# Block 0 of a fused sparse-attention and feed-forward kernel: a written list of steps in place of due times, and local outputs joined by row

## The chip, the core and the metric

The kernel runs on one core of a Trainium2 chip, in one launch. The metric is the device time of that launch in microseconds, as the median of several runs. Lower is better. The engines are PE (matrix products, transposes), DVE and ACT (elementwise work, copies out of PSUM, exponentials), POOL (masks at the start) and SP, whose queue issues nearly all transfers. Each engine works through its own list of instructions in order and waits where an operand isn't ready.

## The reference

Attention over 8 batches, 8 heads, 576 positions and 64 dimensions, with a local mask in half the heads and a strided one in the other half; the heads are joined to rows of 512 and go through a feed-forward layer with a SiLU gate.

```python
rel = pos[:, None] - pos[None, :]
mask_local = (rel >= 0) & (rel < 32)
mask_strided = (rel >= 0) & (pos[None, :] % 32 == pos[:, None] % 32)
masks = np.stack([mask_local if h < H // 2 else mask_strided for h in range(H)], axis=0)
scores = np.where(masks, q @ k.T / 8, -1e9)
attn = softmax(scores)                  # along the keys
x = (attn @ v).transpose(0, 2, 1, 3).reshape(4608, 512)
h = x @ w_in                            # 512 x 2048
g = h * (1.0 / (1.0 + np.exp(-h)))
return g @ w_out                        # 2048 x 512
```

All of it is float32.

## The kernel before

**Blocks and chunks.** The 4608 rows of x go in 9 blocks of 512 columns (x is held transposed: 128 partitions are two heads of 64). For each block the hidden layer goes in 16 chunks of 128. A chunk is 12 products into one PSUM bank (`hidden`, four column pieces of x times three pairings) and 12 into the four output banks (`output`). Three pairings, since each float32 operand is split into a rounded high half and the rest (`w` high and low, `xhi` and `xlo`, `ghi` and `glo`), and high times high, high times low and low times high are added up. A chunk's hidden bank goes through a tanh on ACT and a gate on DVE, and then through its own split.

**Attention groups.** Each batch is cut into six groups: three local ones (12 tiles of 32 queries against 64 keys, two heads) and three strided ones (8, 8 and 6 tiles). Group numbers run on: 0 to 5 make the x of batch 0, 6 to 11 that of batch 1, and so on. A group's steps are: load k and q (`k`), scores on PE (`S`), masked peak on DVE (`M`), exponentials with row sums on ACT (`E`), row sums inverted on DVE (`R`), scaling on DVE (`N`), transposes on PE (`T`), a copy out of PSUM (`P`), load v (`v`), values on PE (`O`), a copy into x (`B`). In the trace, exponentials are L425, peaks L416, scaling L437, transposes L443, values L472, scores L398.

**Block 0 is special.** While the first block of the feed-forward layer runs, the kernel must also load all weights and split them (32 pieces of 256 or 512 KB: `p` load, `a` two roundings on ACT, `j` join on DVE, `b` high half by DVE or ACT, `d` low half on DVE), make the x of batch 0 and batch 1 and score groups 12 and 13. Chunk fc of block 0 has steps `h` and `i` (the two halves of `hidden`), `t` (tanh), `g` (gate), `w` and `l` (high and low half of the gated value), `o` (`output`). `H` and `L` split x into `xhi` and `xlo`: H00 to H03 for block 0, H10 to H13 for block 1. All these steps are put into lists for the engines by a planner that runs when the program is built, not on the chip.

**The planner.** Each step has a cost per engine that may do it, a due time, steps that it comes after, and rings of buffers that it takes. `Steps.arrange` repeats: take the steps that could start, keep those that start within 0.05 of the earliest, and choose the one with the least due time; the engine is the one on which the step would end first. Where PE would stand idle, `keep_warm` adds transposes of the identity (L664) whose results nobody reads. Due times are formulas, such as

```python
outs = [attention_steps(c, (5 + 2.4 * c, 9 + 2.4 * c, 11 + 2.4 * c, 13 + 2.4 * c))
        for c in range(NG)]
begin, pace = 24.0, 6.4
```

**Blocks 1 to 8** are written as a plain loop over chunks: `hidden`, `silu`, the `output` of the chunk before, and at three chunks of a block `products`, which computes the values of two groups and the scores of the two groups behind them. There the transposes are done by DVE in blocks (`turn_by_blocks`, L462), not by PE. For block 1 the three chunks are 2, 6 and 11, for the later ones 1, 6 and 11; groups 12 and 13 are normalised and turned in chunks 0 and 1 of block 1 (`following`). `store` scales the four output tiles of a block by 0.5 and writes them out.

## Time and profile before

| | |
|---|---|
| time, median of 3 runs | 888.8 us (888.44 to 888.88) |
| the profiled execution | 889.7 us, its span 887.6 us |
| PE busy | 876.9 us (99%) |
| DVE busy | 509.1 us (57%) |
| ACT busy | 314.2 us (35%) |
| HBM read, written | 54.00 MB, 9.44 MB |
| first product of h0 (PE, L554) | starts at 29.50 us |
| first products of block 1 (PE, L554) | start at 135.77 us in the chain |

The profile is one execution. Its span is 2.1 us shorter than the time of that execution, which holds the launch's beginning and end too. PE's busy time counts overlapping products, so 99% does not mean that every product runs at its best. An engine's idle time is named with what ended it, and only idle time on the way to the last instruction makes the kernel longer.

### The profile page before, as it was taken

The numbers are of one execution on the slowest core, as the hardware profiler recorded it, in microseconds if no ns is written. First come the engines' busy times: TensorE is split into PE (matmuls) and PEld (weight loads), VectorE is DVE, ScalarE is ACT, GpSimd is POOL, SyncE is SP. The second block draws the span as 40 slices with busy tenths as digits, with TensorE's granted clock in tenths as the row PEclk, the third lists the DMA queues.
The fourth block names the chain that finished last, engine by engine and source line by source line (L and its number), as shares of the span: only waits on it lengthen the run. The fifth ranks groups of instructions, "written<-read, shape, count | busy, mean of one in ns | idle before, by whom it ended". The sixth has DMA issues, their size and how long they took to land.

```text
span 887.6 us, 18081 instructions
## 1 busy us (share of the span) xinstructions
PE 876.9 (99%) x7283; PEld 722.0 (81%) x7283; DVE 509.1 (57%) x1602; ACT 314.2 (35%) x1059; POOL 5.8 (1%) x28
## 2 busy tenths in 40 slices
PE   8999999999999999999999999999999999999998
PEld 7777788888888887888888888888788888888886
DVE  5999757666476566458556656655654433343333
ACT  6989643333333333314413432333331221121111
POOL 2000000000000000000000000000000000000000
PEclk9999999999999999999999999999999999999999
DMA  8886513122122202202301221221200010001001
GB/s 267 280 272 222 164 45 111 58 71 76 49 68 71 75 36 81 71 1 75 116 7 64 76 70 46 71 75 48 68 29 1 1 48 1 0 1 48 1 0 48
DMA packets 37043, 64.60 MB, mean 73 GB/s; under 512 B 2912, under 2 KB 23776, under 8 KB 36960
## 3 DMA queue, kind: packets, MB, share of 16 engines
q1 hardware_dynamic: 36000, 62.60, 21.6%
q8 instruction: 57, 0.93, 0.4%
q10 hardware_dynamic: 960, 0.85, 0.3%
q14 instruction: 26, 0.21, 0.1%
HBM read 54.00 MB, written 9.44 MB: 71 GB/s over the span
## 4 chain that ended last, share of the span: by engine, by line
PE 90%; DVE 5%; DMA 3%; ACT 1%; issue 0%; SPq 0%; ACTq 0%; DVEq 0%
PE po L600 42%; PE ps L554 41%; PE ps L398 3%; PE ps L487 3%; DMA stage<-w_in 2%; DMA stage<-w_out 1%; DVE stage L293 1%; DVE w L337 1%; PE ps L472 1%; PE po L472 1%; DVE w L333 0%; PE ps L664 0%; DVE glo L580 0%; DMA k<-kqt 0%; DVE th L568 0%
## 5 line engine op out<-in xcount | busy, mean ns | idle before, releaser
L554 PE MATMUL ps<-xhi,w 128*128 128x512 f32 x1152 | 378.1, 391 | 0.1
L568 DVE SCALAR_TENSOR_TENSOR th<-th,ps 128x512 f32<-128x512 f32 (+1 forms) x147 | 99.3, 676 | 272.7 <-ACT th L564 272.6
L554 PEld LDWEIGHTS ps<-xhi,w 128*128 128x128 f32 x1152 | 216.3, 188 | 45.6 <-DVE w L337 0.4
L564 ACT ACTIVATE th<-ps 128x512 f32<-128x512 f32 (+1 forms) x147 | 86.5, 588 | 455.1 <-PE ps L554 448.8
L554 PE MATMUL ps<-xlo,w 128*128 128x512 f32 x576 | 224.2, 389 | 0.0
L600 PE MATMUL po<-w,ghi 128*128 128x512 f32 x504 | 157.1, 393 | 0.4 <-DVE ghi L576 0.4
L554 PEld LDWEIGHTS ps<-xlo,w 128*128 128x128 f32 x576 | 108.1, 188 | 22.0
L600 PEld LDWEIGHTS po<-w,ghi 128*128 128x128 f32 x504 | 93.5, 188 | 20.4 <-ACT stage L287 0.8
L425 ACT ACTIVATE sm<-sm,sums 128x64 f32<-128x64 f32 x320 | 106.4, 338 | 3.1 <-DVE sums L416 3.1
L580 DVE TENSOR_TENSOR glo<-th,ghi 128x512 fp32r<-128x512 f32 (+1 forms) x147 | 100.0, 681 | 11.8
L600 PE MATMUL po<-w,glo 128*128 128x512 f32 x252 | 98.5, 391 | 1.6 <-DVE sums L416 0.9
L600 PE MATMUL po<-stage,ghi 128*128 128x512 f32 x288 | 88.7, 389 | 0.0
L600 PE MATMUL po<-v,ghi 128*128 128x512 f32 x216 | 67.3, 393 | 0.1
L576 DVE CAST ghi<-th 128x512 fp32r<-128x512 f32 (+1 forms) x140 | 59.0, 422 | 11.8
L600 PEld LDWEIGHTS po<-stage,ghi 128*128 128x128 f32 x288 | 54.1, 188 | 11.2
L425 ACT ACTIVATION_READ_ACCUMULATOR sm<-sm,sums 128x1 f32 x320 | 61.4, 192 | 0.0
L462 DVE STREAM_TRANSPOSE pt<-sm 32x192 f32<-32x192 f32 (+1 forms) x144 | 56.4, 392 | 2.6
L600 PEld LDWEIGHTS po<-w,glo 128*128 128x128 f32 x252 | 47.3, 188 | 12.9 <-DVE glo L580 1.7
L600 PE MATMUL po<-stage,glo 128*128 128x512 f32 x144 | 56.0, 389 | 0.0
L600 PEld LDWEIGHTS po<-v,ghi 128*128 128x128 f32 x216 | 40.1, 188 | 8.8 <-issue 0.3
L600 PE MATMUL po<-k,ghi 128*128 128x512 f32 x144 | 44.4, 390 | 0.0
L600 PE MATMUL po<-v,glo 128*128 128x512 f32 x108 | 42.2, 391 | 0.2 <-DVE glo L580 0.2
(72 smaller groups left out, 664.6 us busy)
## 6 DMA issues: line engine op xcount, KB each, us to landing
out<-stage SPq DMA_DIRECT2D x36, 256.0 KB, 2.0
v<-vt SPq DMA_DIRECT2D x21, 384.0 KB, 5.4
k<-kqt SPq DMA_DIRECT2D x14, 512.0 KB, 4.8
stage<-w_out SPq DMA_DIRECT2D x14, 512.0 KB, 4.2
stage<-w_in SPq DMA_DIRECT2D x12, 512.0 KB, 4.5
k<-kqt SPq DMA_DIRECT2D x14, 416.0 KB, 4.0
v<-vt SPq DMA_DIRECT2D x14, 256.0 KB, 5.0
k<-kqt SPq DMA_DIRECT2D x7, 448.0 KB, 3.9
```

The source lines that it names most:

```text
L293: nc.vector.scalar_tensor_tensor(out=upper, in0=upper, scalar=3, in1=lower, op0=ALU.logical_shift_left, op1=ALU.bitwise_or,)
L398: nc.tensor.matmul(self.pss[h][rows, c * KW : (c + 1) * KW], kbd[at, 1, g.q0[t] : g.q0[t] + g.rows], kbd[at, 0, g.k0[t] : g.k0[t] + KW], s ...
L425: nc.scalar.activation(out=self.s_sb[:, c, h], in_=self.s_sb[:, c, h], func=AF.Exp, bias=self.peaks[:, c, h : h + 1], scale=-1.0, accum_ou ...
L462: nc.vector.transpose(out=pt[to, r % 2], in_=src[rows, 1 - r % 2])
L472: nc.tensor.matmul(self.pso[h * D : (h + 1) * D, t * size : (t + 1) * size], vbd[at, t], moved, start=True, stop=True,)
L487: nc.tensor.matmul(self.pso[p][h * D : (h + 1) * D, i * size : (i + 1) * size], vbd[at, 2 * i + h], moved, start=True, stop=True,)
L554: nc.tensor.matmul(ph, weight(0, wi, fc)[:, cc * P : (cc + 1) * P], x[xi][cc], start=(cc, n) == (0, 0), stop=(cc, n) == (NP - 1, 2),)
L564: nc.scalar.activation(out=th[:, cols], in_=ph[:, cols], func=AF.Tanh, scale=0.5)
L568: nc.vector.scalar_tensor_tensor(out=th[:, cols], in0=th[:, cols], scalar=1.0, in1=ph[:, cols], op0=ALU.add, op1=ALU.mult,)
L576: copy[engine](out=g[0][:, cols], in_=th[:, cols])
L580: nc.vector.tensor_sub(out=g[1][:, cols], in0=th[:, cols], in1=g[0][:, cols].bitcast(F32))
L600: nc.tensor.matmul(po[tt], g[gi][:, cols], weight(1, wi, fc), start=fc == 0 and n == 0, stop=fc == NFC - 1 and n == 2,)
```

## The change

**A written list.** A string `PLAN` names the 439 steps of block 0 in an order, some with an engine behind a dot (`P0.D` is DVE, `P4.A` is ACT). A new method `follow` makes each step's place in the list its due time and takes away the other engines. `arrange` then runs as before; on each engine the steps come out in the list's order. The planner's costs for PE's fillers rise (0.27 to 0.34 up to time 12 rather than 9), so that fewer are put in: 29 transposes instead of 75.

**Local outputs by row.** In batches 0 and 1 the exponentials of local groups are no longer scaled (`N` goes for them). The values step puts queries on PSUM partitions, with one bank for each head, stationary 32 columns of `pt` and moving 64 columns of `vbd`. A new step `Q` (`share`) multiplies the two banks by the inverted sums on DVE into an SBUF tile `xq`; `X` (`back`) turns it on PE with three transposes; `B` copies it into x.

**Smaller edits.** Groups 12 and 13 are normalised and turned in the list (`V12`, `V13`), and the first `products` of block 1 comes at chunk 1. The second half of `v0` is issued by SP, not ACT. In the last block's `store`, even tiles are scaled whole by DVE and odd ones whole by ACT, where before each was cut in two halves. The dependences of `h`, `i`, `o`, `H` and of lent buffers are written out more fully, since due times no longer imply them.

```diff
+PLAN = """
+k0 k1 k2 S0 M0 k4 S1 E0 M1 v0 S2 M2 k3 E1 T0 S4 P0.D R0 v1 M4 E2 O0 T1 Q0 k5 P1.D X0 R1 S3 E4
...
+H12.A j31 H13.D b31.A L12 L13 d31 i15 o14 t15 g15 w15.D l15
+"""
...
-COLD, WARM = 0.27, 0.14
-WARM_FROM, WARM_UNTIL = 9.0, 60.0
+COLD, WARM = 0.34, 0.14
+WARM_FROM, WARM_UNTIL = 12.0, 60.0
...
+    def follow(self, plan):
+        for i, word in enumerate(plan.split()):
+            name, _, engine = word.partition(".")
+            step = self[name]
+            step.due = i
+            step.costs = {e: c for e, c in step.costs.items() if e.startswith(engine)}
...
         def values(self):
             g, pt, vbd = self.g, self.pt, self.vbd
-            self.pso, size = self.bank("pso"), STRIDE if g.local else SEQ
+            if g.local:
+                self.pso = [self.bank("pso") for _ in range(2)]
+            else:
+                self.pso = self.bank("pso")
             for t, c, rows in self.tiles:
                 r = rows.start // STRIDE
                 for h in range(2):
                     at = slice(h * KW, (h + 1) * KW)
-                    moved = pt[at, c, r] if g.local else pt[at, c, r : r + 2, :HALF]
-                    nc.tensor.matmul(
-                        self.pso[h * D : (h + 1) * D, t * size : (t + 1) * size],
-                        vbd[at, t], moved, start=True, stop=True,
-                    )
+                    if g.local:
+                        nc.tensor.matmul(
+                            self.pso[h][rows, c * D : (c + 1) * D],
+                            pt[at, c, r], vbd[at, t], start=True, stop=True,
+                        )
+                    else:
+                        nc.tensor.matmul(
+                            self.pso[h * D : (h + 1) * D, t * SEQ : (t + 1) * SEQ], vbd[at, t],
+                            pt[at, c, r : r + 2, :HALF], start=True, stop=True,
+                        )
...
+        def share(self):
+            g = self.g
+            self.xq = att.tile([P, 3 * P], F32, name="xq", bufs=1)
+            o_sb = self.xq.rearrange("p (c h d) -> p c h d", h=2, d=D)[:, : g.n]
+            for h, o_ps in enumerate(self.halves(self.pso)):
+                inv = self.rsum[:, :, h].unsqueeze(2).broadcast_to([P, g.n, D])
+                nc.vector.tensor_mul(o_sb[:, :, h], o_ps, inv)
+        def back(self):
+            self.psx = self.bank("psp")
+            for c in range(self.g.n):
+                at = slice(c * P, (c + 1) * P)
+                nc.tensor.transpose(self.psx[:, at], self.xq[:, at], ident)
...
-            half = DM if k < NBLK - 1 else DM // 2
-            nc.scalar.mul(out=osb[:, :half], in_=po[tt][:, :half], mul=0.5)
-            if half < DM:
-                nc.vector.tensor_scalar_mul(osb[:, half:], po[tt][:, half:], 0.5)
+            if k == NBLK - 1 and tt % 2 == 0:
+                nc.vector.tensor_scalar_mul(osb, po[tt], 0.5)
+            else:
+                nc.scalar.mul(out=osb, in_=po[tt], mul=0.5)
...
-        soft = add(f"N{c}", {"DVE": 0.08 + 0.13 * n}, t1 - 1, [r], a.scale)
+        soft = e
+        if not local or a.b >= EARLY:
+            soft = add(f"N{c}", {"DVE": 0.08 + 0.13 * n}, t1 - 1, [r], a.scale)
         if last == "S":
+            t = add(f"V{c}", {"DVE": 0.85 + 0.45 * n}, t1, [soft], a.turn_by_blocks, takes=["pt"])
...
         if local:
-            d = add(f"B{c}", {"ACT": 0.38, "DVE": 0.47}, t2 + 1, [o],
-                    lambda: a.done(d.engine), gives=[o])
+            q = add(f"Q{c}", {"DVE": 0.53}, t2 + 0.5, [o, r], a.share, takes=["xq"], gives=[o])
+            x = add(f"X{c}", {"PE": 0.1 + 0.12 * n}, t3 + 0.01, [q], a.back, takes=[mid])
+            d = add(f"B{c}", {"ACT": 0.38, "DVE": 0.47}, t3 + 1, [x], lambda: a.done(d.engine),
+                    gives=[x])
...
+    steps.follow(PLAN)
     for step in steps.arrange():
         step.act()
...
-        plan[(b - 1) * NFC + (1 if b > 2 else 2, 6, 11)[at // 2]] = c
+        plan[(b - 1) * NFC + (1, 6, 11)[at // 2]] = c
...
-    for i in range(2):
-        group = groups[2 * NG + i]
-        following[NFC + i] += [lambda g=group: normalize(g), group.turn_by_blocks]
```

In the rows that follow, `sm` holds a group's exponentials, `po` and `ps` are PSUM banks, `pt` turned exponentials, `xb` x, `stage` a weight piece; `x18` at the end counts equal rows. ACT at the start of the program, before (L425 exponential, L525 and L447 copies of local outputs and of turned exponentials, L542 a half of x, L519 a strided output, L282 the first rounding of weights):

```order
L425 ACTIVATE sm,sums<-sm,sums 128x64 x18
L525 COPY xb<-po 128x384
L447 COPY pt<-po 128x384
L425 ACTIVATE sm,sums<-sm,sums 128x64 x8
L525 COPY xb<-po 128x384
L542 CAST xhi<-xb 128x512
L425 ACTIVATE sm,sums<-sm,sums 128x64 x14
L519 COPY xb<-po 128x24x18
L282 ACTIVATE stage_468<-stage_468 128x512
```

and with the change (L453 exponential, L475, L579 and L563 the copies, L312 and L317 the roundings):

```order
L453 ACTIVATE sm,sums<-sm,sums 128x64 x40
L475 COPY pt<-po 128x512
L312 ACTIVATE stage_456<-stage_456 128x512
L317 ACTIVATE stage_456<-stage_456 128x512
L579 COPY xb<-po 128x3x4x32
L563 COPY xb<-po 128x8x18
L563 COPY xb<-po 128x15x18
L475 COPY pt<-po 128x384
L312 ACTIVATE stage_537<-stage_537 128x512
```

The 40 exponentials of the first six groups stood in three pieces with copies of local outputs between them; now they stand in one piece, and all copies come behind it.

DVE soon behind the third group's peaks, before (L433 and L434 row sums, L437 scaling, L447 copy of turned exponentials):

```order
L437 TENSOR_TENSOR sm<-sm,sums 128x384
L433 TENSOR_SCALAR sums<-sums 128x6
L434 RECIPROCAL sums<-sums 128x6
L447 COPY pt<-po 128x384
L437 TENSOR_TENSOR sm<-sm,sums 128x384
```

and with the change, from the peaks of group 4 on (L547 the new scaling of outputs, L461 and L462 row sums, L475 copy of turned exponentials, L579 copy into x):

```order
L547 TENSOR_TENSOR xq<-po,sums 128x3x64 x2
L475 COPY pt<-po 128x384
L461 TENSOR_SCALAR sums<-sums 128x6
L462 RECIPROCAL sums<-sums 128x6
L579 COPY xb<-po 128x3x4x32
```

The scaling of exponentials is gone for local groups; instead the outputs are scaled behind the values, and the copy into x stands behind PE's transposes of them.

PE ahead of the first half of chunk 5, with the values step of group 6, before (L443 transposes, L398 scores, L472 values, L554 a product of `hidden`):

```order
L443 MATMUL ps<-ident,sm 128x128 x4
L398 MATMUL ps<-k_80 32x64 x24
L472 MATMUL ps<-pt,v_77 64x32 x24
L554 MATMUL ps<-xhi,w_0_694 128x512
L554 MATMUL ps<-xlo,w_0_694 128x512
```

and PE between the second half of chunk 4 and o3, with the values step of group 8, with the change (L608 a product of `hidden`, L570 transposes back, L503 values, L654 a product of `output`):

```order
L608 MATMUL ps<-xlo,w_0_645 128x512
L608 MATMUL ps<-xhi,w_0_668 128x512
L570 MATMUL ps<-ident,xq 128x128 x3
L503 MATMUL ps<-v_77,pt 32x64 x24
L654 MATMUL po<-w_0_745,ghi 128x512
L654 MATMUL po<-w_0_761,ghi 128x512
```

The values step has 32 stationary and 64 moving columns instead of the reverse, and transposes of `xq` appear, here those of group 6.

More of the change, by code (lines that the diff above doesn't have):

```diff
@@ L698, in x_steps @@
     def x_steps(k, x, cc, after, due):
-        high = add(f"H{k}{cc}", {"ACT": 0.55, "DVE": 0.38}, due, after,
+        before = [steps[f"H{k}{cc - 1}"]] if cc else []
+        high = add(f"H{k}{cc}", {"ACT": 0.55, "DVE": 0.38}, due, [*before, *after],
                    lambda: x_high(k, x, cc, high.engine))
@@ L725, in gated_low @@
             g_low(state["th", fc], state["g", fc])
-        ha = add(f"h{fc}", {"PE": 1.4}, due, [split_at[0, fc], lows[1], steps["S5"]], first,
+        before = [steps[f"h{fc - 1}"]] if fc else lows[:2]
+        ha = add(f"h{fc}", {"PE": 1.4}, due, [split_at[0, fc], *before], first,
                  takes=["ps", "ph"])
-        hb = add(f"i{fc}", {"PE": 1.4}, due, [ha, lows[3]], second)
+        hb = add(f"i{fc}", {"PE": 1.4}, due, [ha, *lows], second)
         t = add(f"t{fc}", {"ACT": 0.5}, due - 5, [hb], turn, takes=["th"])
```

60 lines of the change are left out of this document (41 added, 19 removed).

## The prediction

> **What bounds the kernel now.** I read the page's busy times and chain first, then busy time by stretch, then the rows of PE, ACT and DVE in order of time. Busy time of an engine, and the chain by engine:
>
> ```profile
> PE 876.9 (99%) x7283; PEld 722.0 (81%) x7283; DVE 509.1 (57%) x1602; ACT 314.2 (35%) x1059; POOL 5.8 (1%) x28
> ...
> PE 90%; DVE 5%; DMA 3%; ACT 1%; issue 0%; SPq 0%; ACTq 0%; DVEq 0%
> ```
>
> PE fills the span, and 90% of the chain is PE. So a change gains what it takes off PE's queue or out of PE's waits. Busy time by stretch (PE, PEld, DVE, ACT, POOL, granted clock, DMA share, GB/s):
>
> ```profile
> 0.00:25.00 25.00, 22.33 (x478) 19.10 (x479) 14.23 (x102) 16.43 (x84) 5.77 (x28) 1.00 0.85 268
> 25.00:50.00 25.00, 24.45 (x241) 19.64 (x240) 24.05 (x74) 22.76 (x63) 0.00 (x0) 1.00 0.85 286
> 50.00:75.00 25.00, 23.92 (x228) 18.47 (x226) 24.31 (x73) 21.02 (x49) 0.00 (x0) 1.00 0.87 278
> 75.00:100.00 25.00, 24.93 (x271) 20.18 (x268) 21.00 (x62) 20.78 (x64) 0.00 (x0) 1.00 0.56 175
> 100.00:125.00 25.00, 24.81 (x170) 19.95 (x169) 15.70 (x29) 12.24 (x23) 0.00 (x0) 1.00 0.25 83
> ```
>
> Only block 0 is not plain PE. In 25 to 75 us DVE is as full as PE (24.05 and 24.31 of 25), ACT nearly, and the transfers take 0.85 to 0.87. Two things matter: when PE begins the dense products, and what PE carries from there to block 1. The rows of PE around the beginning:
>
> ```profile
> 28.67 0.91 PE L472 MATMUL po<-pt,v 64*64 64x54 f32 x24
> ...
> 29.50 0.51 PE L554 MATMUL ps<-xhi,w 128*128 128x512 f32 x1
> ```
>
> At 29.50 the first h0 product starts, directly behind the last values step; that is the end of the head. Why so late is seen on ACT (last column: idle time before, and who ended it):
>
> ```profile
> 5.92 0.35 ACT L425 ACTIVATE sm<-sm,sums 128x64 f32<-128x64 f32 x1 [0.97 <-DVE sums L416]
> ...
> 11.57 0.33 ACT L425 ACTIVATE sm<-sm,sums 128x64 f32<-128x64 f32 x1
> ...
> 14.16 0.48 ACT L525 COPY xb<-po 128x384 f32<-128x384 f32 x1 [2.16 <-PE po L472]
> ...
> 19.51 0.48 ACT L525 COPY xb<-po 128x384 f32<-128x384 f32 x1 [1.74 <-PE po L472]
> ...
> 25.20 0.89 ACT L519 COPY xb<-po 128x432 f32<-128x432 f32 x1
> ```
>
> The 40 exponentials of the first six groups start at 5.92 and end at 25.20, though each takes 0.33 us from start to start (18 of them, back to back, from 5.92 to 11.57 + 0.33). ACT stood 2.16 and 1.74 us behind two copies of local outputs that waited for PE's values, and 22 exponentials stood queued behind these copies. DVE tells the same:
>
> ```profile
> 9.04 0.23 DVE L416 CUSTOM_DVE_ANT_0 sm<-ps,mask_local 128x64 f32<-128x64 f32 x1 [0.79 <-PE ps L398]
> ...
> 10.34 0.56 DVE L437 TENSOR_TENSOR sm<-sm,sums 128x384 f32<-128x384 f32 x1
> ...
> 16.79 0.56 DVE L525 COPY xb<-po 128x384 f32<-128x384 f32 x1 [1.79 <-PE po L472]
> ...
> 25.33 0.17 DVE L433 TENSOR_SCALAR sums<-sums 128x6 f32<-128x6 f32 x1 [0.86 <-ACT sm L425]
> ...
> 29.42 0.69 DVE L337 TENSOR_TENSOR w<-stage,w 128x512 fp32r<-128x512 f32 x1
> ```
>
> 1.79 us of DVE's idling is again for local values, 0.86 for the last exponentials; the low half of the first weight piece, which h0's third product reads, ends at 30.02.
>
> **The change part by part.** I sum against the profiled execution, 889.7 us (span 887.6); the median of the runs, 888.8, is 0.9 us lower, and I take the difference off the median.
>
> *Head.* The new list puts the 40 exponentials in one run: 5.92 + 40 x 0.332 = 19.2 us instead of 25.2. Then ACT no longer sets h0; DVE does. Busy time by stretch, from the first peak of the third group to the end of that low half (step d0):
>
> ```profile
> 9.04:30.02 20.98, 19.62 (x434) 17.20 (x434) 16.42 (x88) 17.04 (x76) 0.00 (x0) 1.00 0.92 298
> ```
>
> DVE is busy 16.4 of 20.98 us and idles 4.6. Up to the same step the new list drops the scaling of three local groups (the 10.34 row; its 0.56 overlaps its neighbours, 0.47 from start to start), two copies of turned weights (0.6 and 0.47) and one join (0.6), together 3.1; it adds three scalings of outputs, two copies (0.47 each) and one cast (0.34). The output scaling is not in the trace: two instructions of 192 columns out of PSUM. It lies between 0.47, the old scaling of 384 columns, and 0.84, twice the 0.42 us that 256 columns out of PSUM take in the rows of the end below; I take 0.53, near the first since the elements are the same. That is 2.9 for 3.1. The third group's peaks cannot start much before 9.04, so d0 ends at 9.04 + 16.4 - 0.2 = 25.2 if DVE never waits, against 30.02. Of the idle 4.6, 2.65 are the two waits shown, which the new order moves away. Of the rest I leave 0.9: d0 ends near 26.2, and h0, whose first two products don't need it, starts at 26.0. **3.5 us earlier**; 4.3 (no wait) and 1.5 (most waits stay) are the ends. The transfers must keep up: v0 now goes behind k4, and k0 to k2, k4 and v0 are 2.2 MB, 8.3 us at the 268 GB/s of the first stretch, so the first values step may wait some tenths past 10 us (in the 0.9). The first weight piece is wanted by 20 us and has one transfer fewer ahead of it (v3 goes behind p1): nothing; if it is late, that is part of the 1.5.
>
> *From h0 to block 1.* The chain in order of time shows where block 1's first twelve products start (start, length):
>
> ```profile
> 135.77 2.95 PE ps L554 x12
> ...
> 141.44 2.72 PE ps L554 x12
> ```
>
> From 29.50 to 135.77 PE spends 106.3 us. Both lists hold the same 31 x 12 products there, 2.72 us each twelve when undisturbed, 0.23 more right behind small products. Rows of PE for what differs (local values are L472 with 64x32, local scores L398 with 64*32, transposes L443, warm-up transposes L664):
>
> ```profile
> 31.19 0.82 PE L664 MATMUL ps<-ident 128*128 128x128 f32 x6
> ...
> 32.06 0.50 PE L554 MATMUL ps<-xhi,w 128*128 128x512 f32 x1
> ...
> 36.30 1.26 PE L664 MATMUL ps<-ident 128*128 128x128 f32 x10
> ...
> 37.31 0.47 PE L554 MATMUL ps<-xhi,w 128*128 128x512 f32 x1
> ...
> 46.47 0.49 PE L443 MATMUL ps<-ident,sm 128*128 128x128 f32 x3
> ...
> 46.71 0.48 PE L554 MATMUL ps<-xhi,w 128*128 128x512 f32 x1
> ...
> 55.58 0.70 PE L600 MATMUL po<-w,ghi 128*128 128x512 f32 x2 [0.43 <-DVE ghi L576]
> ...
> 56.69 0.50 PE L600 MATMUL po<-w,glo 128*128 128x512 f32 x1 [0.41 <-DVE glo L580]
> ...
> 59.63 0.72 PE L398 MATMUL ps<-k 64*32 64x64 f32 x48
> ...
> 60.28 1.59 PE L472 MATMUL ps<-pt,v 64*64 64x32 f32 x48
> ...
> 61.80 0.50 PE L554 MATMUL ps<-xhi,w 128*128 128x512 f32 x1
> ```
>
> Three local values steps, 60.28 to 61.80 = 1.52 us each. The new form writes the two heads to two banks, with 32 stationary and 64 moving columns: this is the shape of the local scores, 59.63 to 60.28 = 0.65. Ends are 0.65 and 1.52; I take 0.65, since shape and bank use are those of the score row. That removes 2.6 us. Each group's three transposes back (46.47 to 46.71 = 0.24) come three times, once with a change of its own (0.23): adds 1.0. Warm-up steps fall from 6 + 10 transposes (0.87 and 1.01) to 3, some 0.5: minus 1.4. S6 now lies behind h0: 0.65 and part of a change, plus 0.8. PE's waits, 0.43 and 0.41 and smaller ones, make 1.08 in 50 to 75 us and 0.26 up to 125 (by the table of stretches): 1.3.
>
> What waits come instead? Each DVE step stands in PE's way only if it is late. Up to l5, the new DVE list holds 54 joins, low halves, gates and remainders of 0.60, 19 casts of 0.34, 11 peak steps (11.0), 11 totals of 0.42, and 8.9 of copies and scalings: 63.3 us, so at the head's offset (26.2 less 16.2 and less 1.8 for the first two groups' peaks = 8.2) l5 ends at 71.5. PE reaches o5 after 16 x 1.36 + 5 x 2.72 of products, 8.8 of scores, values and transposes, 0.5 of warm-up and 12 changes at 0.2: 47.1 us behind h0, at 73.1. Slack 1.6 us, as much as DVE idled in 25 to 75 us (0.95 + 0.69): short waits at most. I take 0.7 us of waits, 0 and 3 as ends: minus 0.6. Sum of this part: -2.6 + 1.0 - 1.4 + 0.8 - 0.6 = **-2.8 us**.
>
> Joining the local outputs by row puts a new round trip, DVE, PE, then a copy, ahead of x, but x of block 0 is due only with DVE's list above, and x of block 1 at the end of block 0 where DVE is 63% busy (15.70 of 25). The normalising and turning of groups 12 and 13 moves there from block 1; from the page's costliest groups (busy, mean ns):
>
> ```profile
> L462 DVE STREAM_TRANSPOSE pt<-sm 32x192 f32<-32x192 f32 (+1 forms) x144 | 56.4, 392 | 2.6
> ```
>
> Twelve such block transposes and four short steps are some 6 us, under 9.3 us of DVE idle per 25: nothing; if they spilled, nothing yet, since block 1's first use of them is more than a chunk away. Block 1's products of PE stay as they are, one chunk earlier.
>
> *Queues.* SP issues k4 ahead of v0, pieces 5, 7, 11 ahead of 4, 6, 10. SP's waits on weight stages are for DVE to free them:
>
> ```profile
> SPq L329 <- DVE w L337: 17.6, 6, 4.3
> ```
>
> So a faster DVE starts transfers earlier; at 0.85 there is room for it, and the pieces come in the order in which the list converts them. v0's second half moves from ACT's queue to SP's: 0.6 us of issue, ahead of E0 by far.
>
> *End.* The last tile was scaled in two halves, ACT then DVE, one behind the other:
>
> ```profile
> 883.79 0.38 ACT L612 ACTIVATE stage<-po 128x256 f32<-128x256 f32 x1 [0.25 <-PE po L600]
> ...
> 884.21 0.42 DVE L614 TENSOR_SCALAR stage<-po 128x256 f32<-128x256 f32 x1 [0.21 <-ACT stage L612]
> ...
> L612 ACT ACTIVATE stage<-po x36: 384/598/604, 139.4 to 883.8; 128x512 f32<-128x512 f32 x32, 128x256 f32<-128x256 f32 x4
> ```
>
> Now it is one ACT instruction of 0.60 instead of 884.63 - 883.79 = 0.84: **-0.2**.
>
> Sum: -3.5 - 2.8 - 0.2 = -6.5, so 888.8 - 6.5 = **882.3 us**.
>
> **The clock.** Warm-up transposes fall from 75 to 29. Early ones are slow, late ones fast:
>
> ```profile
> 1.36 2.61 PE L664 MATMUL ps<-ident 128*128 128x128 f32 x11 [1.36 <-POOL ident masks.py:199]
> ...
> 22.07 1.04 PE L664 MATMUL ps<-ident 128*128 128x128 f32 x8
> ```
>
> 2.61 / 11 = 0.24 us against 1.04 / 8 = 0.13, though the granted clock reads 1.00 in every stretch; fewer fillers might leave PE slow for longer, which is rival 3. [...]
>
> **Rivals.**
> 1. *The lead is lost to supply* (20%). DVE, ACT and transfers are full from 25 to 75 us; if in-order stalls on DVE of 5 us together eat the slack of 1.6, PE waits at o3 to o6 and the head's 3.5 is worth nothing to speak of. For it: DVE 99% busy, waits at 55.58 and 56.69. Against: PE's new order puts more hidden products ahead of o5. 888.8 - 2.8 - 0.2 = 885.8.
> 2. *No change* (6%). Local values keep 1.52 in the new form (+2.6 behind h0), and in the head, where three of them stand on DVE's way, the lead shrinks to 1.5 (+2.0), with 0.5 more of waits: 882.3 + 5.1 = 887.4. Against: the score row.
> 3. *Slower: the clock stays low* (6%). If the thinned fillers keep PE at 0.24 instead of 0.13 through the head, the small products between 10.5 us and h0 (two scores, six values and nine transposing steps, 9.5 us, an estimate by the rows above) double; some 4 us of that falls into PE's idle time, and the first 4 us of dense products double too: +9.5 us, 891.8. It decides from 6.5 us of such loss on. Against: S1, T0 and O0 still keep PE at work.
> 4. That the list isn't followed I exclude: the rows of the new order stand as listed.
>
> **How the numbers follow.** The forecast holds 68%: 880.0 (head -4.3, waits 0, and 0.9 of smaller switches) to 884.2 (head -1.5). Eight in ten take in half of rival 1, up to 886.0, and the low end with waits at nothing, 879.7. Two runs of one kernel here differ by up to 0.44 us; 0.2%, 1.8 us, is what I call a change. Faster: forecast and rival 1, 0.88; same 0.06; slower 0.06.
>
> **What would show it.** Right: ACT's exponentials one run to about 19.5; first h0 product at 25.2 to 27; local values 0.65 to 0.75; block 1's first product near 129.5; PE's waits in 30 to 85 below 1.5 us. Wrong: DVE idle on PE's values or transposes for over 2 us in the head; PE waiting for remainders or weight halves at o3 to o6; transposes above 0.2 us past 15 us.

## The result, and the profile after

The changed kernel takes **879.57 us** (median of four runs, 878.97 to 880.85), against 888.84 us for the kernel before on the same chip: a ratio of 0.989, 95% interval 0.9875 to 0.9904. That is 9.3 us, where 6.5 were forecast; 879.57 lies just below the forecast's low end of 879.7. The profiled executions are 889.7 and 879.7 us (spans 887.6 and 877.6), so 10.0 us apart, and the profile of before was 0.9 us above its median.

The page of the changed kernel: busy times, and the chain by engine.

```profile
PE 868.6 (99%) x7255; PEld 714.4 (81%) x7255; DVE 506.0 (58%) x1601; ACT 315.0 (36%) x1062; POOL 5.7 (1%) x28
...
PE 97%; DVE 1%; DMA 1%; ACT 0%; issue 0%; ACTq 0%
```

DVE has left the chain (5% before, 1% now). Busy time by stretch, in the same columns as before (PE, PEld, DVE, ACT, POOL, granted clock, DMA share, GB/s):

```profile
0.00:25.00 25.00, 20.16 (x461) 15.23 (x461) 15.28 (x110) 17.18 (x87) 5.75 (x28) 1.00 0.86 257
25.00:50.00 25.00, 24.69 (x367) 19.21 (x367) 24.40 (x87) 24.20 (x73) 0.00 (x0) 1.00 0.86 289
50.00:75.00 25.00, 25.00 (x262) 19.93 (x264) 24.81 (x75) 24.50 (x66) 0.00 (x0) 1.00 0.87 296
75.00:100.00 25.00, 25.00 (x267) 20.09 (x259) 23.81 (x89) 21.41 (x70) 0.00 (x0) 1.00 0.37 123
```

Between 25 and 100 us DVE is still full, yet PE no longer waits: 25.00 of 25 in the third and fourth stretch, where it was 23.92 and 24.93.

I cut both executions at the same four points, read from PE's rows: the first h0 product (h0 below), the first product of block 1, the last product, the end of the span.

| us | before | after | measured | forecast |
|---|---|---|---|---|
| head: to the first h0 product | 29.50 | 27.20 | -2.3 | -3.5 |
| from there to block 1's first product | 106.20 | 101.62 | -4.6 | -2.8 |
| block 1's first product to the last product | 747.66 | 744.54 | -3.1 | 0 |
| last product to the end | 4.28 | 4.27 | 0.0 | -0.2 |

**The head.** PE's rows of the changed kernel (start, length; in brackets the idle time before and what ended it):

```profile
8.69 0.90 PE L471 MATMUL po<-ident,sm 128*128 128x128 f32 x3
9.52 0.48 PE L426 MATMUL ps<-k 64*64 64x64 f32 x4
11.34 1.12 PE L426 MATMUL ps<-k 64*64 64x64 f32 x28 [1.34 <-DMA k<-kqt]
...
12.79 0.97 PE L503 MATMUL po<-v,pt 64*32 64x64 f32 x48
...
16.36 0.81 PE L471 MATMUL po<-ident,sm 128*128 128x128 f32 x3
```

DVE at that place, and ACT's exponentials, in the same execution:

```profile
12.60 0.22 DVE L444 CUSTOM_DVE_ANT_0 sm<-ps,mask_strided 128x64 f32<-128x64 f32 x1 [2.09 <-PE ps L426]
```

```profile
6.34 0.35 ACT L453 ACTIVATE sm<-sm,sums 128x64 f32<-128x64 f32 x1 [2.05 <-DVE sums L444]
...
12.87 0.35 ACT L453 ACTIVATE sm<-sm,sums 128x64 f32<-128x64 f32 x1 [0.45 <-DVE sums L444]
...
16.75 0.35 ACT L453 ACTIVATE sm<-sm,sums 128x64 f32<-128x64 f32 x1 [1.11 <-DVE sums L444]
...
21.07 0.33 ACT L453 ACTIVATE sm<-sm,sums 128x64 f32<-128x64 f32 x1
```

The exponentials are one run on ACT now, without copies between them, but it goes from 6.34 to 21.40, not from 5.92 to 19.2. It breaks twice for late peaks. The cause of the first break is in the rows: PE stood 1.34 us in the middle of the fourth group's scores for the second half of a load, and DVE stood 2.09 us for these scores. The second break waits for the next peaks, whose scores come behind on PE. The load is k4's. It goes into the buffer that group 0 uses, so SP cannot issue it until S0 has read that buffer, and v0 stands behind it in SP's queue: the issues up to it end at 7.01 us, and v0's begins at 7.05 (SP's rows stand with the exchange below).

The prediction let DVE set h0. DVE from the first peak of the third group (8.78) to the end of the first low half (step d0, 27.31):

```profile
8.78:27.31 18.53, 16.32 (x366) 12.76 (x367) 15.67 (x91) 15.77 (x76) 0.00 (x0) 1.00 0.96 287
```

DVE is busy 15.67 us there and idles 2.86, and h0 starts 0.11 us before that low half ends.

**Block 0 after the head.** A local values step (24 products in the code, 48 in the trace, of 32 stationary by 64 moving columns) from start to start, 38.69 to 39.35:

```profile
38.69 0.72 PE L503 MATMUL ps<-v,pt 64*32 64x64 f32 x48
39.35 0.72 PE L654 MATMUL po<-w,ghi 128*128 128x512 f32 x2
```

It takes 0.66 us where the old form took 1.52. The list of PE's waits from 30 to 85 us (total, times, longest) holds a single line:

```profile
PE ps L608 <- DVE th L622: 0.3, 1, 0.3
```

### The profile page after: what moved, and what is told of

Its sections match the earlier page's. It is cut to its first block, busy times and chain, and to the rows that moved or that the text cites. A ratio compares the mean times of both kernels' runs of the same rounds, so it can differ in the third digit from the quotient of the medians.

```text
span 877.6 us, 18035 instructions
## 1 busy us (share of the span) xinstructions
PE 868.6 (99%) x7255; PEld 714.4 (81%) x7255; DVE 506.0 (58%) x1601; ACT 315.0 (36%) x1062; POOL 5.7 (1%) x28
## 4 chain that ended last, share of the span: by engine, by line
PE 97%; DVE 1%; DMA 1%; ACT 0%; issue 0%; ACTq 0%
PE po L654 45%; PE ps L608 44%; PE ps L426 3%; PE ps L523 3%; DMA k<-kqt 1%; PE ps L508 0%; PE ps L471 0%; PE po L471 0%; PE ps L503 0%; DVE w L367 0%; ACT xb L563 0%; PE po L503 0%; DVE sm L444 0%; DVE sm L465 0%; DVE stage L323 0%
## 5 line engine op out<-in xcount | busy, mean ns | idle before, releaser
L608 PE MATMUL ps<-xhi,w 128*128 128x512 f32 x1152 | 377.0, 390 | 0.3 <-DVE th L622 0.3
L608 PEld LDWEIGHTS ps<-xhi,w 128*128 128x128 f32 x1152 | 216.2, 188 | 45.7 <-DVE th L622 0.4
L608 PE MATMUL ps<-xlo,w 128*128 128x512 f32 x576 | 224.2, 389 | 0.0
L654 PE MATMUL po<-w,ghi 128*128 128x512 f32 x504 | 157.4, 393 | 0.0
L608 PEld LDWEIGHTS ps<-xlo,w 128*128 128x128 f32 x576 | 108.1, 188 | 22.1
L654 PEld LDWEIGHTS po<-w,ghi 128*128 128x128 f32 x504 | 93.3, 188 | 19.8
L453 ACT ACTIVATE sm<-sm,sums 128x64 f32<-128x64 f32 x320 | 106.4, 337 | 3.6 <-DVE sums L444 3.6
L654 PE MATMUL po<-w,glo 128*128 128x512 f32 x252 | 98.2, 390 | 0.0
L654 PE MATMUL po<-stage,ghi 128*128 128x512 f32 x288 | 88.7, 389 | 0.0
L654 PE MATMUL po<-v,ghi 128*128 128x512 f32 x216 | 67.3, 393 | 0.0
L654 PEld LDWEIGHTS po<-stage,ghi 128*128 128x128 f32 x288 | 54.1, 188 | 11.3
L453 ACT ACTIVATION_READ_ACCUMULATOR sm<-sm,sums 128x1 f32 x320 | 61.2, 191 | 0.0
L654 PE MATMUL po<-stage,glo 128*128 128x512 f32 x144 | 56.0, 389 | 0.0
L654 PEld LDWEIGHTS po<-w,glo 128*128 128x128 f32 x252 | 47.3, 188 | 10.1
L654 PEld LDWEIGHTS po<-v,ghi 128*128 128x128 f32 x216 | 40.1, 188 | 8.5
L654 PE MATMUL po<-k,ghi 128*128 128x512 f32 x144 | 44.5, 390 | 0.0
L654 PE MATMUL po<-v,glo 128*128 128x512 f32 x108 | 42.1, 390 | 0.0
```

Source lines behind the costliest of these rows:

```text
L453: nc.scalar.activation(out=self.s_sb[:, c, h], in_=self.s_sb[:, c, h], func=AF.Exp, bias=self.peaks[:, c, h : h + 1], scale=-1.0, accum_ou ...
L608: nc.tensor.matmul(ph, weight(0, wi, fc)[:, cc * P : (cc + 1) * P], x[xi][cc], start=(cc, n) == (0, 0), stop=(cc, n) == (NP - 1, 2),)
L654: nc.tensor.matmul(po[tt], g[gi][:, cols], weight(1, wi, fc), start=fc == 0 and n == 0, stop=fc == NFC - 1 and n == 2,)
```

## Experiments

All kernels were timed in five rounds beside the kernel before. The stages are cut as above, each from one profiled execution; the ratio is to the kernel before on the same chip. A profiled execution can lie off the median of its kernel: 2.6 us above it for the list with the old local form, 1.6 above for 8 more fillers, 1.2 below without the list, up to 1.0 elsewhere. So a few tenths in the head or up to block 1 are no difference; blocks 1 to 8 repeat better, 744.50 to 744.54 us in the six executions of the changed kernel and its variants that show no stall there.

| kernel | median, us | ratio (95%) | head | to block 1 | blocks 1 to 8 |
|---|---|---|---|---|---|
| no list | 888.17 | 0.9976 (0.9966 to 0.9987) | 27.49 | 104.43 | 748.32 |
| list, old local form | 886.49 | 0.9969 (0.9955 to 0.9982) | 31.24 | 103.89 | 747.51 |
| 8 more fillers | 881.18 | 0.9902 (0.9887 to 0.9918) | 26.90 | 103.03 | 746.34 |
| groups 3, 4 exchanged | 877.44 | 0.9862 (0.9844 to 0.9879) | 24.34 | 101.31 | 744.54 |
| before, shifted | 887.44 | 0.9977 (0.9968 to 0.9986) | 29.15 | 106.77 | 744.64 |
| after, shifted | 883.25 | 0.9938 (0.9925 to 0.9951) | 27.03 | 102.23 | 747.44 |
| small edits undone | 879.83 | 0.9889 (0.9875 to 0.9902) | 26.89 | 102.76 | 744.51 |
| after, again | 879.31 | 0.9883 (0.9868 to 0.9897) | 26.58 | 102.65 | 744.51 |
| exchanged, again | 879.15 | 0.9878 (0.9864 to 0.9892) | 25.68 | 102.30 | 744.51 |
| v0 ahead of k4 | 881.18 | 0.9905 (0.9887 to 0.9924) | 25.82 | 103.44 | 744.97 |
| exchanged, v0 ahead of k3 | 882.65 | 0.9914 (0.9898 to 0.9929) | 27.57 | 103.35 | 745.35 |
| fillers ahead of S4 | 880.86 | 0.9905 (0.9890 to 0.9921) | 26.38 | 102.22 | 746.13 |
| exchanged, fillers ahead of S2 | 879.08 | 0.9882 (0.9868 to 0.9895) | 25.98 | 102.17 | 744.50 |

### Which part brings what: the list and the row form

No list (due times order block 0, the row form stays):

```diff
-    steps.follow(PLAN)
```

> The changed kernel without the list: block 0 is ordered by due times again, with the new row form of the local groups and the new filler costs kept. Theory (the list brings the head and the missing waits, the row form the shorter values): the head loses what it gained, h0 at 28.5 to 29.5 instead of 27.20, and some of the waits inside block 0 come back (0.5 to 1.5 us); values stay at about 0.66 us for a local step; blocks 1 to 8 take 744.5 us as in the changed kernel, since its TensorE instruction stream differs from that by 12 fillers only. Time 882 to 883.5. Rival (the row form alone brings it all, the list only repeats what the rule would do): within 0.4 us of 879.6, h0 at 27.0 to 27.5.

The time, 888.17, is above both expectations. The theory missed on the head: h0 is at 27.49, so the change without the list shortens it by 2.0 us, and the list adds 0.3 to 0.9 (27.20 and 26.58 in the changed kernel's two executions). Behind h0 the theory held: block 0 takes 2.8 us longer than in the changed kernel, 1.8 longer than in its second execution (102.65, in the table). PE waits again there:

```profile
PE ps L608 <- DVE pt L475: 1.0, 1, 1.0
PE ps L503 <- ACT pt L475: 0.7, 1, 0.7
PE ps L471 <- ACT sm L453: 0.3, 1, 0.3
```

Blocks 1 to 8 are 3.8 us longer, which no theory expected: block 1 has one wait of 1.97 us for DVE, and the small products that begin at 649.56 us have a stall of 1.37 us of the kind explained below.

The list with the old local form (scaling ahead of the transposes, 64x32 values in one bank, no Q and X; the block transposes of groups 12 and 13 wait for the copies P8 to P11, or the ring of `pt` would run out):

```diff
-... T0 S4 P0.D R0 v1 M4 E2 O0 T1 Q0 k5 P1.D X0 R1 ...
+... R0 N0 T0 S4 P0.D v1 M4 E2 O0 R1 N1 T1 k5 P1.D ...
...
-                    if g.local:
-                        nc.tensor.matmul(
-                            self.pso[h][rows, c * D : (c + 1) * D],
-                            pt[at, c, r], vbd[at, t], start=True, stop=True,
-                        )
...
+                    moved = pt[at, c, r] if g.local else pt[at, c, r : r + 2, :HALF]
+                    nc.tensor.matmul(
+                        self.pso[h * D : (h + 1) * D, t * size : (t + 1) * size],
+                        vbd[at, t], moved, start=True, stop=True,
+                    )
```

> The list kept, the row form undone: the scaling N stands ahead of the transposes again, the local values are products of 64x32 into one bank, and Q and X are gone. Theory: the local values cost 1.5 us instead of 0.66 after h0 (3 steps, +2.6) and the transposes back save 1.04, so h0 to block 1 is 1.2 to 2 us longer than in the changed kernel; the head is within 1 us of 27.20, because the list and not the form sets the order of the exponentials. Time 880.5 to 882.5. Rival (the row form shortens the head's chain, since the scaling no longer stands ahead of the transposes): h0 at 28.5 or later, time 883 to 885.

The rival holds for the head: without the row form it is 31.24 in this execution, worse than before the change. The time, 886.49, is above both expectations, and two stalls of the kind explained below, of 1.55 and 1.53 us, add to it. Two local values steps in the head, on a TensorE that is still slow (0.23 us a transpose), took 5.29 us:

```profile
18.72 5.29 PE L510 MATMUL po<-pt,v 64*64 64x32 f32 x96
...
24.85 2.48 PE L723 MATMUL ps<-ident 128*128 128x128 f32 x11
```

So the head gains by the row form, with or without the list, and in this execution loses 1.7 us with the list alone; between h0 and block 1 the list gains 2.3 us even with the old form. How much of the 31.24 belongs to the old form itself and how much to the slow TensorE, one execution, 2.6 us above its median, does not show.

### Blocks 1 to 8: where the instruction stream is refilled

The chunk code of blocks 1 to 8 is the same on PE in both kernels apart from one chunk's place in block 1. Before, PE stood still there three times: 1.44 and 1.32 us from one product to the next, at 339 and 626 us, and 0.54 at 209. One of the places, in the kernel before:

```profile
336.79 0.72 PE L398 MATMUL ps<-k 64*32 64x64 f32 x48
337.44 1.39 PE L487 MATMUL ps<-pt,v 64*64 64x32 f32 x80
338.65 0.65 PE L398 MATMUL ps<-k 64*64 64x64 f32 x30
340.52 0.33 PE L398 MATMUL ps<-k 64*64 64x64 f32 x2 [1.22 <-issue]
```

Two products of a step that was already running wait 1.22 us for nothing that the profile shows. What runs shortly before is a transfer of instructions; the DMA view of 337 to 341 us has it as its last queue (16 KB; the trace of before has 57 of them for 14,656 records of PE, 257 to one, and the last seven of the changed kernel are 252 to 260 records apart, so I take 256 instructions, an estimate from these counts):

```profile
q8 instruction: 1, 0.02, 2.1%
```

Each cluster of small products in blocks 1 to 6 (three to a block, the last and shorter one left out) is 304 or 320 PE instructions, products and their weight loads, in 2.3 to 2.5 us, more than one such transfer brings. Where a cluster begins in the grid of 256 is set by all instructions ahead of it, and the change takes out 54 (14,602 records of PE instead of 14,656). I moved that place alone. The kernel before, with 50 score products of block 0 done twice (the same result; each is two products and two weight loads in the trace):

```diff
+AGAIN = {(1, 4): 24, (2, 0): 24, (1, 0): 2}
...
+                    if again.get((self.b, self.at), 0):
+                        again[self.b, self.at] -= 1
+                        nc.tensor.matmul(
+                            self.pss[h][rows, c * KW : (c + 1) * KW],
...
```

> The kernel before with 50 score products of block 0 done twice (200 TensorE instructions more, the same result), so that from block 1 on the places at which the instruction stream is refilled fall as in the changed kernel (56 instructions short of a whole block of 256 against before, where the changed kernel is 54 short). Theory (the stream ran dry at 209, 340 and 626 us): none of these gaps is left, and from block 1's first product to the last one it takes 744.5 to 745.2 us instead of 747.66; block 0 takes 0.5 to 2 us longer for the added products; time 886.0 to 888.0. Rival (the 3.1 us come from the two transposing steps and the products that the change moved): 747.4 to 748 us there, time 889.3 to 890.8.

The changed kernel, with 14 products done twice:

```diff
+AGAIN = {(2, 0): 14}
```

> The changed kernel with 14 score products of block 0 done twice (56 TensorE instructions more), so that from block 1 on the refills fall as in the kernel before. Theory: gaps of 0.3 to 1.2 us come back at the same steps as before (near 201, 331 and 616 us), block 1 to the last product takes 746.3 to 747.5 instead of 744.54; time 881.5 to 883. Rival (moved steps): 744.3 to 744.9 there, time 879.5 to 880.3.

Both went as the theory says (the time of the second, 883.25, is 0.3 above its range). With 200 instructions more, the kernel before takes 744.64 us from block 1 to the last product instead of 747.66, and is 2.0 us faster as a whole. The changed kernel loses 2.9 us there. The same place of block 3, first in the kernel before as shifted, then in the changed one as shifted:

```profile
338.57 0.66 PE L402 MATMUL ps<-k 64*64 64x64 f32 x32
339.15 0.73 PE L611 MATMUL po<-w,ghi 128*128 128x512 f32 x2
```

```profile
332.62 0.65 PE L430 MATMUL ps<-k 64*64 64x64 f32 x29
334.23 0.33 PE L430 MATMUL ps<-k 64*64 64x64 f32 x3 [0.96 <-issue]
```

The third run excludes the rival, that the edits of block 1 and of the last block bring it:

```diff
-            if k == NBLK - 1 and tt % 2 == 0:
-                nc.vector.tensor_scalar_mul(osb, po[tt], 0.5)
-            else:
-                nc.scalar.mul(out=osb, in_=po[tt], mul=0.5)
+            half = DM if k < NBLK - 1 else DM // 2
+            nc.scalar.mul(out=osb[:, :half], in_=po[tt][:, :half], mul=0.5)
+            if half < DM:
+                nc.vector.tensor_scalar_mul(osb[:, half:], po[tt][:, half:], 0.5)
...
-        plan[(b - 1) * NFC + (1, 6, 11)[at // 2]] = c
+        plan[(b - 1) * NFC + (1 if b > 2 else 2, 6, 11)[at // 2]] = c
...
+        following[NFC + i] += [lambda g=group: normalize(g), group.turn_by_blocks]
```

> The changed kernel with its small edits undone: the last block's scaling by halves on both engines, the transposes of groups 12 and 13 back in block 1, and the products of block 1 a chunk later. Theory (these edits are beside the path): 879.3 to 880.2; the end after the last product within 0.3 us of 4.27; blocks 1 to 8 within 0.5 us of 744.5. Rival (they are what blocks 1 to 8 gained): 746.5 to 748 us there, time 881.5 to 883.

744.51 us, and 4.26 behind the last product: the small edits are worth nothing that can be seen.

The fifteen executions profiled here (both kernels and thirteen runs) hold 255 such clusters. Fifteen of them show a stall, with 0.44 to 1.61 us from one product to the next where 0.34 is usual, and all fifteen begin at places 125 to 146 of the 256. Of the clusters of 320 instructions, the six that begin there (125 to 137) all stall; of those of 304, nine of the ten that begin at 136 to 146 stall, and none that begins below 136. The other 240 clusters show none, and no cluster that begins outside these places stalls. By these counts one stall was forecast ahead of its run (fillers ahead of S4, below), and it stood where it was forecast.

A finer count of the same records shows where PE stands. In all fifteen the last product ahead of the stall is the 192nd or 193rd record of its 256, and the next one starts 1.2 to 1.6 us after a transfer of instructions has ended. Six more stand-stills, of 0.5 to 1.1 us, lie at this place in the heads of five of the runs here, and end 1.2 to 1.4 us after such a transfer. One of them, in the first values step with groups 3 and 4 exchanged:

```profile
10.40 0.45 PE L503 MATMUL po<-v,pt 64*32 64x64 f32 x31
11.33 0.35 PE L503 MATMUL po<-v,pt 64*32 64x64 f32 x17 [0.48 <-issue]
```

What is not shown is why thirteen clusters of 304 that begin at 127 to 136 get through, though a transfer starts as soon behind their beginning: 1.1 us behind it both in the one at 359.37 us of the changed kernel, without a stall, and in the one at 206.46 of the kernel before, with its 0.54.

In the kernel with fillers ahead of S4 the profile names another releaser:

```profile
361.00 0.54 PE L431 MATMUL ps<-k 64*64 64x64 f32 x24
362.68 0.63 PE L659 MATMUL po<-w,ghi 128*128 128x512 f32 x2 [1.15 <-DVE sums L449]
```

An output step doesn't read `sums`; a name like this one, of an engine that the instruction doesn't depend on, is a sign that the true cause isn't in the list of releasers.

### The head: fillers, loads, and when TensorE turns fast

The filler costs of before in the changed kernel:

```diff
-COLD, WARM = 0.34, 0.14
-WARM_FROM, WARM_UNTIL = 12.0, 60.0
+COLD, WARM = 0.27, 0.14
+WARM_FROM, WARM_UNTIL = 9.0, 60.0
```

> The changed kernel with the filler costs of the kernel before (0.27 us until 9.0 us instead of 0.34 until 12.0): 37 fillers instead of 29. Theory (the fillers stand in waits that are there anyway; those after h0 were what the change saved): 879.3 to 880.6, h0 within 0.4 us of 27.20. Rival (the head fell short of the forecast because TensorE ran slow until 16.5 us for want of fillers): transposes at 0.13 us instead of 0.27 before 15 us and h0 at 26.0 to 26.7, time 878.4 to 879.2.

h0 at 26.90, between the changed kernel's two executions: the fillers don't set the head. The time, 881.18, is above both expectations; the 16 instructions more put two clusters at places 146 and 138, with stalls of 1.61 and 0.44 us.

Groups 3 and 4 exchanged, so that the fourth load has a buffer of its own:

```diff
-k0 k1 k2 S0 M0 k4 S1 E0 M1 v0 S2 M2 k3 E1 T0 S4 P0.D R0 v1 M4 ...
+k0 k1 k2 S0 M0 k3 S1 E0 M1 v0 S2 M2 k4 E1 T0 S3 P0.D R0 v1 M3 ...
```

> The changed kernel with groups 3 and 4 exchanged in the list, with all their steps. k3 goes to a buffer of its own and can be sent at once, while k4 goes to k0's buffer and has to wait on SP until the scores of group 0 have read it; v0 and the third group's load stand behind it in the queue. Theory (that place in SP's queue is what the head lacks against the forecast): the wait of 1.34 us of the fourth scores on their load goes, values of group 0 begin before 12.79 and h0 comes 0.6 to 1.4 us earlier (25.8 to 26.6), time 878.2 to 879.0. Rival (the chain is bound by the exponentials on ScalarE and by DVE, the load is beside it): h0 within 0.3 us of 27.20, time within 0.4 us of 879.6.

Here are SP's issues, first of the changed kernel, then of the exchange, and the fourth scores of the exchange:

```profile
0.73 6.28 SPq L382 DMA_DIRECT2D k<-kqt  x5
7.05 1.07 SPq L387 DMA_DIRECT2D v<-vt  x2
```

```profile
0.73 3.46 SPq L382 DMA_DIRECT2D k<-kqt  x5
4.99 0.83 SPq L387 DMA_DIRECT2D v<-vt  x2
```

```profile
9.51 0.70 PE L426 MATMUL ps<-k 64*64 64x64 f32 x32
```

The five issues take 3.46 us instead of 6.28, the wait of 1.34 us is gone, and h0 comes 2.9 us earlier, more than expected. I then ran it again beside the changed kernel on one chip, with two other orders of the same loads:

> The changed kernel once more, beside the three that follow on the same chip. All theories: h0 at 26.8 to 27.3, block 1 to the last product 744.5 to 744.6 without a gap, time 878.5 to 880.5.

> Groups 3 and 4 exchanged in the list, once more, beside the changed kernel on the same chip. Theory (the gain of 2.9 us in the head is the exchange): 2 to 3 us faster than the changed kernel, h0 at 24.2 to 24.6. Rival (it was the chip or the run): within 0.8 us of it.

The changed kernel repeated (879.31, h0 at 26.58). The exchange did not: 879.15 us, 0.2 us from the changed kernel, and the runs of the two overlap (878.93 to 879.38 against 879.19 to 880.35). In the profiled executions h0 is 0.9 us and block 1's first product 1.25 us earlier (127.98 against 129.23), far from the 3.2 us of the first run.

```diff
-k0 k1 k2 S0 M0 k4 S1 E0 M1 v0 S2 M2 k3 ...
+k0 k1 k2 v0 S0 M0 k4 S1 E0 M1 S2 M2 k3 ...
```

> The changed kernel with one word of the list moved: v0 stands ahead of k4 on SP, so the first values no longer wait for the group that waits for k0's buffer, and on TensorE they come ahead of the fourth scores. Theory (what the head lost is the queue behind that wait): v0 is issued by 5 us instead of 7.05, the first values begin at 9.8 to 10.6 instead of 12.79, h0 at 24.3 to 25.6, time 877.3 to 878.6, although k4 still goes to k0's buffer. Rival (the fourth group's own scores bind, since its exponentials are next in ScalarE's run): h0 at 26.5 to 27.3, time within 0.8 us of the changed kernel.

```diff
-k0 k1 k2 S0 M0 k3 S1 E0 M1 v0 S2 M2 k4 ...
+k0 k1 k2 v0 S0 M0 k3 S1 E0 M1 S2 M2 k4 ...
```

> Groups 3 and 4 exchanged, and v0 ahead of k3 as well. Theory (with fewer loads beside it k0's first half lands 0.3 to 0.4 us sooner, as without the list, where ScalarE's first exponential began at 5.92 instead of 6.33): first exponential at 5.9 to 6.1, h0 0.2 to 0.5 us earlier than with the exchange alone, time 876.8 to 877.4. Rival (the loads of the head are no longer what binds): the same as the exchange alone within 0.3 us.

With v0 ahead of k4, v0 is issued at 3.01 and the first values begin at 10.02, as the theory has it, and the exponentials end at 19.35, where the prediction had them; h0 is at 25.82, 0.2 us behind the theory's range and 0.8 us earlier than in the changed kernel beside it. But from h0 to block 1 it takes 103.44, and PE waits there again:

```profile
PE ps L608 <- DVE th L622: 1.4, 1, 1.4
PE ps L503 <- DVE pt L475: 0.6, 1, 0.6
PE po L654 <- DVE w L367: 0.2, 1, 0.2
```

Block 1's first product comes at 129.26, within 0.1 us of the changed kernel's 129.23. What the head gains there, block 0 gives back on DVE. Behind it a cluster at place 139 adds a stall of 0.55 us; the medians lie 1.9 us apart, of which this accounts for a part only. With both moves the first exponential begins at 5.93 as expected, yet h0 comes at 27.57; the theory of the first loads falls with that.

In the changed kernel PE's three transposes at 16.36 still start 0.24 us apart, and from 18.64 on 0.14. This switch came at 9.5 us in the first run of the exchange, near 13 in the second, and at about 14.7 and 17 in the two of the changed kernel. From the end of the last wait of over 0.3 us ahead of the switch to the switch it was 4.5 us in the first run of the exchange (5.02 to 9.5) and 5.7 in the first of the changed kernel (11.34 to 17), but about 9 with both moves (7.96 to 17, with one wait of 0.29 between), so the 3.5 to 6 us of the next expectation hold for some runs only. Is it the switch to the fast rate that makes the head long? Eight more transposes ahead of S4 keep PE at work while its load is late; four ahead of S2, `{(0, 2): 4}`, were to do the same for the exchange:

```diff
+FILL = {(0, 4): 8}
...
+            for i in range(FILL.get((self.b, self.at), 0)):
+                nc.tensor.transpose(self.pss[0][:, :P], ident, ident)
```

> The changed kernel with 8 more transposes of the identity on TensorE ahead of the fourth scores, into their own bank, so that TensorE works through the wait for their load instead of standing still. Theory (TensorE's switch from 0.24 to 0.137 us a transpose comes some 3.5 to 6 us after its last wait of over 0.3 us, and the late load thus costs more than its own 1.34 us): the switch comes by 11.5 us instead of 14.7 to 17, h0 at 25.0 to 26.0 instead of 26.6 to 27.2, though the load lands no earlier. Rival (the switch comes when it comes, or the exponentials bind): h0 within 0.4 us of 26.6 to 27.2. Beside that the 16 more TensorE instructions move the products of about 360 us to place 145 of the 256, inside 125 to 146, where the earlier runs stalled: a gap of 1.2 to 1.7 us is expected there and nowhere else after block 1's start, so the time is 879.5 to 881.5 by the theory.

> Groups 3 and 4 exchanged in the list, and 4 more transposes ahead of the third scores, where TensorE waited 0.69 us for the peaks of the first group on this kernel's second run. Theory (the head of the exchange hangs on when TensorE switches): the switch by 10.5 us, h0 at 24.2 to 24.9 and not 25.68; the products of about 360 us at place 137, a gap of at most 0.6 us; time 877.0 to 878.8. Rival (h0 depends on something else that differs from run to run): h0 25.2 to 26.2, time 878.8 to 880.

With the fillers ahead of S4 the switch came as expected, inside the fillers themselves:

```profile
9.27 1.30 PE L427 MATMUL ps<-ident 128*128 128x128 f32 x8
...
11.00 0.68 PE L431 MATMUL ps<-k 64*64 64x64 f32 x28 [0.18 <-DMA k<-kqt]
...
17.69 0.56 PE L431 MATMUL ps<-k 64*64 64x64 f32 x20 [0.61 <-DMA k<-kqt]
```

But h0 is at 26.38, 0.2 to 0.8 us earlier than in the changed kernel's two executions, not 1 to 2: a fast TensorE meets the next late load, here k5's. The theory of the switch falls as an account of the head's length. With the exchange, h0 came at 25.98, as the rival has it; there PE waited 1.42 us for the second group's load, more than in any other run, and the switch came near 12 us, not by 10.5, so the theory was not put to the test there. The stall near 360 us was there in the first of the two (1.36 us at place 144), beside one of 0.73 us at place 136 that I had not expected. In the second the cluster near 360 us began at place 136 without a stall; up to 0.6 us had been expected.

## Why the prediction was right in sign and too small

**The change helps, by shorter local values and an earlier, denser block 0: right.** Up to block 1's first product the forecast was 6.3 us, and 6.9 were measured (6.5 in the second execution). That it is so near is in part luck: the head was over-sized and the waits were under-sized. What made the whole too small is a term behind that point, blocks 1 to 8, which the sum put at nothing.

- *Head, -3.5: over-sized.* It measured -2.3 and, in the second execution, -2.9. The path was right: DVE sets h0, with 15.67 us of work from the third group's peaks to d0's end where 16.2 were counted. The step that failed is the idle time, "of the rest I leave 0.9", and with it "the transfers must keep up: ... some tenths past 10 us (in the 0.9)". DVE idles 2.86 us, and 2.09 of them are the wait for the fourth group's scores, whose load the buffer of S0 holds back on SP's queue. In the eleven executions with both the list and the row form this work takes 15.4 to 15.8 us and the idle time lies between 0.3 and 3.0; in nine of them h0 starts within 0.12 us of d0's end, and in the two with v0 moved 0.7 and 0.9 us behind it. The reason for the gain was in part wrong too: I gave it to the list's single run of exponentials; the run without the list shows 2.0 us of it with due times. DVE idle on PE for over 2 us in the head and transposes above 0.2 us past 15 us, which I named as signs of failure, both appeared.
- *Local values, -2.6: right.* 0.66 us against the 0.65 taken from the score row; the end of 1.52 is excluded. *Transposes back, +1.0:* measured 1.04. *Fillers, -1.4:* 1.29. *S6, +0.8:* 0.9.
- *Waits, -0.6: under-sized, -2.6 measured.* That is the time of the 372 dense products of this stage (`hidden` and `output`), 90.26 us before and 87.65 after (88.06 in the second execution). I left 0.7 us of new waits and priced the old ones at the idle time that the profile shows, 1.3 us. A stand-still cost more than that. In the kernel before:

```profile
54.76 0.39 PE L554 MATMUL ps<-xhi,w 128*128 128x512 f32 x1
55.58 0.70 PE L600 MATMUL po<-w,ghi 128*128 128x512 f32 x2 [0.43 <-DVE ghi L576]
56.69 0.50 PE L600 MATMUL po<-w,glo 128*128 128x512 f32 x1 [0.41 <-DVE glo L580]
57.03 0.63 PE L600 MATMUL po<-w,ghi 128*128 128x512 f32 x2
```

  From 54.76 to 57.03 four products take 2.27 us, 1.36 more than four times 0.227 (2.72 / 12), with 0.84 us of idle time. The changed kernel has one wait of 0.3 us in this stage; the first product behind small ones costs the same in both, 0.34 us. The run without the list takes 1.8 to 2.8 us more here than the changed kernel's two executions, so this is the list's share. I had named DVE's slack as 1.6 us and rival 1 for the case that it is eaten: it isn't in the changed kernel, but it is in the kernel with v0 ahead of k4.
- *Blocks 1 to 8, nothing: wrong, -3.1 measured.* This is the step that made the forecast too small: "Block 1's products of PE stay as they are". Their order stays, but not their place in the instruction stream. The two shifted kernels show it both ways, -3.0 and +2.9. This gain is not owed to what the change does: it would be lost again by 56 instructions more.
- *End, -0.2: nothing measured.* The last scaling ends 1.07 us after the last product's start, before 1.26; but the last transfer ends 3.20 us behind it, before 3.02.

Rival 2 (local values keep 1.52) and rival 3 (slow TensorE through the head and on) are excluded for the changed kernel, though in the first profiled execution its transposes turn fast later than before the change (0.24 us apart still at 16.36; in the kernel before 0.11 at 11.38). The kernel with the list and the old form shows a good part of rival 3, with a TensorE slow until 25 to 27 us and h0 at 31.24. No run shows the term of rival 3 that the first 4 us of dense products double: even there the first h0 products start 0.34 and 0.24 us apart (31.24, 31.58, 31.82), as in the changed kernel (0.34 and 0.23). Two readings were a little off: by its row the low half of before ends at 30.11, not 30.02, and over 25 to 75 us DVE is 96 and 97% busy, not 99%.

**Still open.** The head's length differs by 0.6 us between the changed kernel's two executions and by 1.3 between those of the exchange. It goes with DVE's idle time, and in the changed kernel that goes with a load: the fourth scores go on at 11.34 us in one execution and at 10.72 in the other, and DVE idles 2.86 and 2.32 us. I did not find what sets the landing of the first loads. Whether the exchange of groups 3 and 4 is faster is not settled: 0.9862 on one chip, 0.9878 beside the changed kernel's 0.9883 on another. No version tried here is shown to beat the changed kernel.

## What to carry over

When a kernel is bound by TensorE and has clusters of small products, look for idle time of a microsecond that ends in "issue", or in an engine that the instruction doesn't read: it can be the instruction stream, and an edit far ahead can move it (here 200 and 56 PE instructions more in block 0 changed blocks 1 to 8 by -3.0 and +2.9 us). Counting the records showed it: the stand-stills here all lie behind the 192nd or 193rd record of the 256. Price a wait from start to start of the products around it, not by the idle time alone (1.36 against 0.84 us in the rows above). A gain in one stage must be read at the next point where everything meets (here block 1's first product), since an earlier start can be given back to a full DVE (with v0 ahead of k4, h0 0.8 us earlier and block 1 at 129.26 instead of 129.23). In a written order, follow every load's buffer: a load that waits for a reader holds all that stands behind it on its queue (v0 was issued at 7.05 us behind k4, at 3.01 ahead of it).

## What the hardware showed unexpectedly

- PE stood still at one place of its instruction stream: of 255 clusters of 304 or 320 instructions in 2.3 to 2.5 us, 15 had 0.44 to 1.61 us from one product to the next, only for starts at places 125 to 146 of the 256, and always behind the 192nd or 193rd record, until 1.2 to 1.6 us after a 16 KB transfer of instructions had ended.
- TensorE's transposes of 128x128 went from 0.21 us apart to 0.11 at 10.7 us in the kernel before, by 9.5 in the first run of the exchange and by 27 in the list with the old local form, while the granted clock read 1.00 in every stretch of the first 30 us of the kernel before and of the changed one, and 0.999 and 1.00 as the means of the other two.
- 48 products of 32 stationary by 64 moving columns into two banks take 0.66 us, and 48 of 64 by 32 into one bank 1.52 us, for the same arithmetic.
